# One decode step of attention with a gated MLP: how the K cache is laid over the 128 partitions, and what the score matmuls read

## The chip, the cores and the metric

The kernel runs on one core of one Trainium2 chip. The metric is device time in microseconds (us) of one execution, lower is better. The time of the kernel before is the median of three runs. Besides, one execution was recorded by the hardware profiler; its span is counted from the first to the last instruction of the core, and its own device time is a little longer than its span.

The names of the engines are those of the profile: PE is the matrix engine, PEld its weight loads, DVE the vector engine, ACT the scalar engine, POOL the GpSimd engine, and SP the engine that here only issues DMAs. A DMA is carried out by up to 16 DMA engines of the core, each of which works through its share of the DMAs in the order in which they were issued on a queue.

## The reference, cut to what matters

Two inputs x of width 448 (a batch of 2, one token each) are normalised, and then

```python
W = 2048                                    # the last 2048 of 8192 cached positions
q = (xn @ wq)                               # 16 heads of 256; each K/V head serves 2 of them
scores = einsum("bhqd,bhkd->bhqk", q, k) * 256 ** -0.5
p = softmax(scores)
s = einsum("bhqk,bhkd->bhqd", p, v) reshaped to 4096, @ wo
g = silu(relu(xn @ w1) @ w2)
out = x + s * g
```

All arrays are bf16. There are 2 batches with 8 K/V heads each, and of each the K and the V window is 2048 x 256, or 1 MB. K and V are 33.6 MB of the 44.1 MB that the kernel reads. Each number read is used for a handful of multiplications.

## The kernel before, in words

**Units.** The 16 pairs of batch and K/V head are handled in four units `u`; a unit has one batch and 4 heads, so 4 MB of K and 4 MB of V. `unit_src` (L197) describes the source of a unit: the 2048 positions of a head are cut into 32 blocks `kb` of 64 positions, and a row of 32 KB is one block of one head. The rows are listed as "kb h (t d)": the outer count is 32 blocks, the inner one 4 heads. So partition p of the SBUF buffer holds block p div 4 of head p mod 4. One DMA loads K of a unit (`load_k`, L279), one loads V (`load_v`, L282). The DMAs go out through `_Prog.dma` (L37), so in the profile all their issues have line L37.

**From K to scores.** `do_T` (L312) transposes K on DVE in four pieces of 128 x 2048 words of 4 bytes (a word is two bf16); the transposition is done in blocks of 32 x 32 words (L315). What was the partition within a group of 32 becomes the column within a block of 32 words. `do_S` (L318) then computes the scores of the unit with 32 matmuls: 8 parts `gp` of the head dimension by 4 heads `h`. The four heads write to four groups of 32 output rows, so that four matmuls can be in the array side by side. The moving operand of one matmul is 512 columns, picked from the transposed tile: 64 steps of 256 elements (`TS`), and within each 8 elements. With the order "block, head" within 32 partitions, the 8 blocks of one head stand 4 words, 16 bytes, apart.

**The rest of a unit.** `ch_max` (L330) finds the maximum over the scores and takes the exponential on ACT, `ch_spread` redistributes the result with 16 matmuls, `ch_pt` builds the weights on DVE, `do_PV` (L363) multiplies with V in 32 matmuls, also four side by side, whose moving operand is contiguous. `do_o_pe`, `do_at_exp` and `do_at` turn the output of the unit into columns for the last product.

**Buffers and what waits for them.** There are two buffers for K (`kbuf`), two for the transposed K (`kt`), and one for V (`vbuf`). `wq` is loaded into `kt[1]`, `w1` and `w2` into `kt[0]` once the scores of unit 2 are done, V of unit 2 into `kbuf[0]`, and `wo` into `kbuf[1]` in five parts. Each engine executes its own list in the order in which it is written out by hand from L466 on. The list of SP, which is the order of the large DMAs, is: wq, K0, K1, V0, K2 (waits for the transposes of unit 0), K3 (for those of unit 1), V1 (for the product with V0), V2 (for the transposes of unit 2), w1 (for the scores of unit 2), V3 (for the product with V1), w2, and five parts of wo (for the transposes of unit 3). SP stands at a DMA until its wait is over, and what is behind it on SP waits too. x is read by two small DMAs that ACT issues: `x_sb` as 2 rows, and `x_c` (L204) as 8 rows of 224 bytes, whose source is listed as 4 quarters by 2 batches. The output goes back in the same form of 8 rows (L549).

**The end.** The output product with `wo` is done in 32 steps on PE (L532 to L544) as the parts of wo land, after which two DVE instructions make the output, and one DMA writes it.

Of the kernel before, what the change touches and what calls it, by code (L numbers as in the profile page):

```python
# [12 lines left out]
PE, DVE, ACTE, SP, POOL = "pe", "dve", "act", "sp", "pool"  # L13
# [68 lines left out]
def bass_recurrent_scan__sliding_block_cached__dense_activation_relu__decode_kernel(  # L82
# [12 lines left out]
    _, HKV, SK, DH = A_k_cache.shape  # L95
# [3 lines left out]
    W = min(4096, max(256, SK // 4))  # L99
# [5 lines left out]
    HU = 4  # L105
    TS = 64
# [10 lines left out]
    with es:  # L117
        pr = _Prog(nc, es)

        def named(name, shape, dt):  # L120
            return es.enter_context(nc.sbuf_tensor(name, shape, dt))
# [4 lines left out]
        def view(t, off, dims, n=128, p0=0, pstep=1):  # L126
            width = t.shape[1]
            return bass.AP(t, p0 * width + off, [[width * pstep, n]] + dims)
# [40 lines left out]
        kbuf = [named(f"kbuf{i}", [128, UW], BF) for i in range(2)]  # L169
        vbuf = named("vbuf", [128, UW], BF)  # L170
        kt = [named(f"kt{i}", [128, UW], BF) for i in range(2)]
# [14 lines left out]
        def mm(out_ap, lhsT, rhs, start, stop=False, **kw):  # L186
            return lambda e: e.matmul(out_ap, lhsT=lhsT, rhs=rhs, start=start, stop=stop,  # L187
                                      skip_group_check=True, **kw)
# [8 lines left out]
        def unit_src(u, cache):  # L197
            hf, b = divmod(u, 2)
            return cache[b, HU * hf:HU * hf + HU, SK - W:SK, :].rearrange("h (kb t) d -> kb h (t d)", t=TS)
# [12 lines left out]
        d_k, d_v = {}, {}  # L212
# [64 lines left out]
        st = {}  # L277

        def load_k(u, deps=()):  # L279
            d_k[u] = pr.dma(SP, kbuf[u % 2][:, :], unit_src(u, A_k_cache), deps)  # L280

        def load_v(u, deps=()):  # L282
            d_v[u] = pr.dma(SP, vhome[u][:, :], unit_src(u, A_v_cache), deps)
# [27 lines left out]

        def do_T(u, c):  # L312
            src, dst = kbuf[u % 2][:, :].bitcast(F32), kt[u % 2][:, :].bitcast(F32)
            deps = [d_k[u], st.get(("S", u - 2))] + ([st["q_mm"]] if u == 1 else [])
            st["T", u] = pr.op(DVE, lambda e: e.transpose(  # L315
                dst[:, 2048 * c:2048 * c + 2048], src[:, 2048 * c:2048 * c + 2048]), deps)

        def do_S(u):  # L318
            deps = [st["T", u], st["q"], st.get(("exp", u - 2)), *st["q_n"]]
            for gp in range(NG):  # L320
                for h in range(HU):
                    lo = (u * NG + gp) * 32 + 8 * h
                    o = pr.op(PE, mm(sbk[u % 2][32 * h:32 * h + 8, :], q_big[:, lo:lo + 8],
                                     view(kt[u % 2], 64 * (gp // 2) + gp % 2 + 2 * h, [[256, TS], [8, 8]]),
                                     gp == 0, gp == NG - 1, tile_position=(0, 32 * h)), deps)
                    deps = []
            st["S", u] = o
# [136 lines left out]


        load_k(0)  # L466
        load_k(1)
        do_q()
        for c in range(4):
            do_T(0, c)  # L470
        do_S(0)
        load_v(0)
        load_k(2, [st["T", 0]])
        for c in range(3):
            do_T(1, c)
        ch_max(0)
        ch_spread(0)
        do_T(1, 3)
        load_k(3, [st["T", 1]])
        ch_pt(0)  # L480
        do_PV(0)
        load_v(1, [st["PV", 0]])
        do_S(1)
        for c in range(3):
            do_T(2, c)
# [5 lines left out]
        do_o(0)  # L491
        ch_pt(1)
        do_S(2)
        for c in range(3):
            do_T(3, c)
# [35 lines left out]
        deps = [st["at", 3], st["fs"]]  # L531
        for j in range(32):  # L532
            deps = deps + [d_wo.get(j)]
            if j < WO_TILED:
                m_o = tiled(j, at2[:, 32 * j:32 * j + 17], wo_sb[:, j * D:(j + 1) * D], WO_TILED, deps)
                deps = []
# [3 lines left out]
            for i in range(4):  # L540
# [3 lines left out]
                deps = []  # L544
# [36 lines left out]
```

## Time and profile before

| what | value |
|---|---|
| time, median of 3 runs (lowest, highest) | 112.09 us (111.26, 112.58) |
| the profiled execution: its device time | 111.33 us |
| the profiled execution: its span | 109.9 us |
| mean granted clock of PE, as a share of full speed | 0.812 |
| HBM read, and its mean rate over the span | 44.11 MB, 402 GB/s |
| PE busy, DVE busy, ACT busy | 62%, 54%, 11% of the span |

How to read it: the profiled execution is 0.76 us under the median of the three runs, and 1.43 us of its device time lie outside the span. "Busy" adds up the instructions of an engine; matmuls that run side by side are pipelined, so a busy PE says only that at least one is under way. In the timeline each row is a group of instructions of one line: the start, the busy time of the group, the engine, the line, the operation, output and inputs, shape, count, and in brackets the idle time just before it with what ended it. In the DMA view a packet is one contiguous run moved by one DMA engine, here one row of a partition, or the 4 bytes with which a DMA engine reports that its share of a DMA is done.

### The profile page before, as it was taken

Reading aid. Unit: us, or ns where it says so; the run is one execution under the profiler, and the core shown is the slowest. Engines: PE = TensorE matmul, PEld = TensorE weight load, DVE = VectorE, ACT = ScalarE, POOL = GpSimd, SP = SyncE. Lnnn points to the kernel's source line nnn. Section 1 sums busy time; section 2 is a strip of 40 time slices with the busy share of each in tenths; the row PEclk is TensorE's granted clock in tenths of the full one; section 3 lists DMA queues with packets and bytes.
Section 4 is the critical chain, followed back from the end, with each engine's and each line's share of the span. In section 5 each row is a group of like instructions: output and inputs, shape, how many; then the busy total and the mean of one; then the engine's idle time right before and its main releaser. Section 6 shows DMA issues by size and latency. Waiting matters only on the chain.

```text
span 109.9 us, 1131 instructions
## 1 busy us (share of the span) xinstructions
PE 68.5 (62%) x490; PEld 23.3 (21%) x469; DVE 59.8 (54%) x84; ACT 12.2 (11%) x21; POOL 4.4 (4%) x14
## 2 busy tenths in 40 slices
PE   0010699500001995579995699989999892556871
PEld 0000001000000110553110622146213841211330
DVE  2167000399999996825984879995005026003621
ACT  2930000340000000201000200040001300020000
POOL 7800000000000000000000000000000000000000
PEclk9999999995555599656999755999999999955555
DMA  6798998999899989989999999999899998999920
GB/s 168 334 460 388 513 430 382 418 489 430 382 501 441 394 382 525 430 382 406 483 430 394 430 489 406 394 477 447 344 425 496 453 406 363 413 433 417 413 115 1
DMA packets 2463, 44.16 MB, mean 402 GB/s; under 512 B 282, under 2 KB 412, under 8 KB 924
## 3 DMA queue, kind: packets, MB, share of 16 engines
q1 hardware_dynamic: 2432, 44.11, 94.3%
q8 instruction: 3, 0.05, 0.2%
q10 hardware_dynamic: 28, 0.01, 0.0%
HBM read 44.11 MB, written 0.00 MB: 402 GB/s over the span
## 4 chain that ended last, share of the span: by engine, by line
DMA 36%; PE 32%; DVE 26%; issue 2%; ACT 1%; SPq 0%
DMA kbuf<-in_A_wo_dram 26%; PE sp L187 23%; DVE kt L315 15%; DMA kt<-in_A_wq_dram 10%; PE sp L192 6%; DVE q_t L305 2%; DVE mx L332 2%; DVE q_big L307 2%; PE gbk L187 2%; ACT e_sb L339 1%; PE hbk L187 1%; DVE q_n L299 1%; DVE pt L356 1%; DVE mxt L334 1%; DVE nb L338 1%
## 5 line engine op out<-in xcount | busy, mean ns | idle before, releaser
L187 PE MATMUL sp<-kt,q_big 128*8 128x512 bf16 x128 | 30.1, 1088 | 14.4 <-DVE kt L315 14.4
L315 DVE STREAM_TRANSPOSE kt<-kbuf 128x2048 f32<-128x2048 f32 x16 | 35.6, 2274 | 2.8 <-DMA kbuf<-in_A_k_cache_dram 2.7
L187 PEld LDWEIGHTS sp<-kt,q_big 128*8 128x8 bf16 x128 | 4.7, 103 | 34.0 <-issue 18.4
L187 PE MATMUL sp<-e_sb,sel 128*128 128x64 bf16 x64 | 8.1, 294 | 5.3 <-ACT e_sb L339 5.3
L187 PE MATMUL sp<-vbuf,pt 128*16 128x512 bf16 x96 | 8.0, 492 | 2.4 <-DMA vbuf<-in_A_v_cache_dram 1.9
L187 PEld LDWEIGHTS sp<-e_sb,sel 128*128 128x128 bf16 x64 | 7.0, 119 | 8.2 <-ACT e_sb L339 8.2
L339 ACT ACTIVATE e_sb<-sp,nb 128x512 bf16<-128x512 f32 x4 | 2.8, 688 | 51.5 <-DVE nb L338 51.5
L332 DVE TENSOR_REDUCE mx<-sp 128x1 f32<-128x512 f32 x4 | 2.7, 687 | 9.4 <-PE sp L187 9.4
L192 PE MATMUL sp<-kt,xr 128*128 128x512 bf16 x21 | 7.7, 488 | 0.0
L299 DVE TENSOR_SCALAR q_n<-sp 128x1024 bf16<-128x1024 f32 x1 | 1.2, 1225 | 10.5 <-PE sp L192 10.5
L187 PE MATMUL sp<-kt,xr 128*128 128x512 bf16 x7 | 3.6, 512 | 3.7 <-DMA kt<-in_A_wq_dram 3.7
L187 PE MATMUL mbk<-ident,xg 2*128 2x2 bf16 x7 | 0.3, 163 | 7.9 <-DVE xg L237 7.9
L356 DVE TENSOR_TENSOR pt<-sp,hmask 128x512 bf16<-128x512 f32 x4 | 2.8, 698 | 4.2 <-PE sp L187 4.2
L387 DVE TENSOR_TENSOR at_exp<-mbk,qmask 128x64 bf16<-128x64 f32 x4 | 0.8, 204 | 7.2 <-PE mbk L187 7.2
L187 PEld LDWEIGHTS sp<-vbuf,pt 128*16 128x16 bf16 x96 | 3.1, 120 | 7.0 <-DMA vbuf<-in_A_v_cache_dram 3.7
L372 ACT ACTIVATE o_sb<-sp 128x512 bf16<-128x512 f32 x4 | 2.4, 593 | 17.9 <-PE sp L187 17.9
L399 DVE TENSOR_SCALAR at<-mbk,rs 64x32 bf16<-64x32 f32 x4 | 1.4, 350 | 3.6 <-PE mbk L187 3.6
L187 PEld LDWEIGHTS sp<-kt,xr 128*128 128x128 bf16 x7 | 0.8, 121 | 10.7 <-issue 6.9
L187 PE MATMUL gbk<-kbuf,at 128*17 128x448 bf16 x24 | 3.0, 570 | 0.1
L302 ACT ACTIVATE q_n<-sp 128x1024 bf16<-128x1024 f32 x1 | 1.0, 1024 | 14.5 <-PE sp L192 14.5
L187 PE MATMUL gbk<-kt,h_sb 128*17 128x448 bf16 x14 | 1.7, 569 | 1.3 <-DMA kt<-in_B_w_dram 1.3
L305 DVE STREAM_TRANSPOSE q_t<-q_n 128x2048 bf16<-128x2048 bf16 x1 | 2.3, 2311 | 0.0
(74 smaller groups left out, 45.8 us busy)
## 6 DMA issues: line engine op xcount, KB each, us to landing
kbuf<-in_A_k_cache_dram SPq DMA_DIRECT2D x4, 4096.0 KB, 17.9
vbuf<-in_A_v_cache_dram SPq DMA_DIRECT2D x3, 4096.0 KB, 21.6
kbuf<-in_A_v_cache_dram SPq DMA_DIRECT2D x1, 4096.0 KB, 18.7
kt<-in_A_wq_dram SPq DMA_DIRECT2D x1, 3584.0 KB, 11.2
kt<-in_B_w_dram SPq DMA_DIRECT2D x2, 1568.0 KB, 19.3
kbuf<-in_A_wo_dram SPq DMA_DIRECT2D x2, 1120.0 KB, 27.3
kbuf<-in_A_wo_dram SPq DMA_DIRECT2D x1, 672.0 KB, 29.3
kbuf<-in_A_wo_dram SPq DMA_DIRECT2D x1, 448.0 KB, 29.1
```

What stands on the lines that cost most here:

```text
L187: return lambda e: e.matmul(out_ap, lhsT=lhsT, rhs=rhs, start=start, stop=stop, skip_group_check=True, **kw)
L192: return lambda e: e.add_instruction(mybir.InstMatmult(name=nc.get_next_instruction_name(), start_tensor_calc=start, stop_tensor_calc=stop ...
L299: e.tensor_scalar(out=view(q_n, 0, [[64, 16], [32, 2], [1, 32]]), in0=view(sp, 0, [[64, 16], [1, 2], [2, 32]]), scalar1=SCALE, scalar2=Non ...
L305: v = pr.op(DVE, lambda e: e.transpose(q_t[:, :], q_n[:, :]), halves)
L307: st["q"] = pr.op(DVE, lambda e, qd=qd: e.tensor_copy(view(q_big, qd, [[NG * 32, NU], [32, NG], [4, 8]], n=32, p0=32 * qd), view(q_t, 0, [ ...
L315: st["T", u] = pr.op(DVE, lambda e: e.transpose(dst[:, 2048 * c:2048 * c + 2048], src[:, 2048 * c:2048 * c + 2048]), deps)
L332: v = pr.op(DVE, lambda e: e.tensor_reduce(out=mx[:, 0:1], in_=sbk[k], axis=AX.X, op=ALU.max), [st["S", u], p_mx, st.get("mxt")])
L334: v = st["mxt"] = pr.op(DVE, lambda e: e.transpose(mxt[:, :], mx[:, :]), [v, st.get("neg")])
L339: st["exp", u] = pr.op(ACTE, lambda e: e.activation(e_sb[k][:, :], sbk[k], ACT.Exp, bias=nb[k][:, 0:1], accum_out=ssum[k][:, 0:1]), [v, st ...
L356: st["pt", u] = pr.op(DVE, lambda e: e.tensor_tensor(out=view(pt[u % 2], 0, [[128, 4], [1, 128]]), in0=view(sp, 1024, [[0, 4], [1, 128]]), ...
L372: st["osb", u] = pr.op(ACTE, lambda e: e.activation(o_sb[:, :], obk[:, :], ACT.Copy), [o, st.get(("oT", u - 1))])
L399: st["at", u] = st["mbk"] = pr.op(DVE, lambda e: e.tensor_scalar(out=view(at2, 16 * b, [[32, 32]], n=64, p0=p0), in0=mbk[p0:p0 + 64, 32:64 ...
```

## The change

K of a unit is loaded by four DMAs in place of one, each to 32 partitions. Within each quarter of 32 partitions the order is now head, then block: partition 32 q + 8 h + j holds block 8 q + j of head h. The transposes wait for all four. The score matmuls pick the columns accordingly: the 8 blocks of one head stand 1 word, 4 bytes, apart, and heads 8 words apart. The bytes that are loaded, the number of matmuls and their shapes, the transposes, V and everything behind the scores stay as they are.

```diff
         def load_k(u, deps=()):
-            d_k[u] = pr.dma(SP, kbuf[u % 2][:, :], unit_src(u, A_k_cache), deps)
+            hf, b = divmod(u, 2)
+            src = A_k_cache[b, HU * hf:HU * hf + HU, SK - W:SK, :].rearrange("h (q kb t) d -> q h kb (t d)", q=4, t=TS)
+            d_k[u] = [pr.dma(SP, kbuf[u % 2][32 * q:32 * q + 32, :], src[q], deps) for q in range(4)]
...
         def do_T(u, c):
             src, dst = kbuf[u % 2][:, :].bitcast(F32), kt[u % 2][:, :].bitcast(F32)
-            deps = [d_k[u], st.get(("S", u - 2))] + ([st["q_mm"]] if u == 1 else [])
+            deps = [*d_k[u], st.get(("S", u - 2))] + ([st["q_mm"]] if u == 1 else [])
...
                     o = pr.op(PE, mm(sbk[u % 2][32 * h:32 * h + 8, :], q_big[:, lo:lo + 8],
-                                     view(kt[u % 2], 64 * (gp // 2) + gp % 2 + 2 * h, [[256, TS], [8, 8]]),
+                                     view(kt[u % 2], 64 * (gp // 2) + gp % 2 + 16 * h, [[256, TS], [2, 8]]),
                                      gp == 0, gp == NG - 1, tile_position=(0, 32 * h)), deps)
```

The source of one such DMA, `src[q]`, is listed as 4 heads by 8 blocks by a row of 32 KB: its outer count is 4. That of the one DMA before, from `unit_src`, is 32 blocks by 4 heads by a row of 32 KB: its outer count is 32.

## The prediction

> **What bounds the kernel now.** I read the page's slices and DMA queues first, then stretches of the span, then the DMA view of short windows, and last the timeline around the scores. The slices and queues of the page:
>
> ```profile
> PEclk9999999995555599656999755999999999955555
> DMA  6798998999899989989999999999899998999920
> ...
> DMA packets 2463, 44.16 MB, mean 402 GB/s; under 512 B 282, under 2 KB 412, under 8 KB 924
> ...
> q1 hardware_dynamic: 2432, 44.11, 94.3%
> ...
> q10 hardware_dynamic: 28, 0.01, 0.0%
> ```
>
> The mean share of the 16 DMA engines is 0.8 or more from the third slice to the last but two. By stretches (start to end, length, busy time of PE, PEld, DVE, ACT, POOL, then PE clock, DMA share, GB/s) it is plainer:
>
> ```profile
> 26.00:36.00 10.00, 0.71 (x4) 0.10 (x8) 9.97 (x6) 0.00 (x0) 0.00 (x0) 0.50 0.98 423
> 52.00:62.00 10.00, 7.87 (x43) 1.85 (x36) 8.26 (x8) 1.03 (x3) 0.00 (x0) 0.99 1.03 441
> 62.00:72.00 10.00, 10.00 (x66) 3.37 (x68) 8.86 (x10) 0.00 (x0) 0.00 (x0) 0.67 1.02 439
> ```
>
> PE is idle in the first and full in the last of these, and the DMA engines are full in all three: they set the pace. The timeline gives the price of one load:
>
> ```profile
> 11.96 0.61 PE L187 MATMUL sp<-kt,xr 128*128 128x512 bf16 x1 [3.71 <-DMA kt<-in_A_wq_dram]
> ...
> 50.65 6.70 DVE L315 STREAM_TRANSPOSE kt<-kbuf 128x2048 f32<-128x2048 f32 x3 [2.72 <-DMA kbuf<-in_A_k_cache_dram]
> ```
>
> PE waited for wq until 11.96, DVE for K2 until 50.65. Between them the engines moved K0, K1, V0 and K2, four loads of 4.19 MB: 38.7 us, or **9.67 us a load**, which is 27.1 GB/s for each of 16 engines.
>
> How many engines a load uses shows in its completion packets. A window that holds the end of just one load, K1 (25 to 35 us):
>
> ```profile
> DMA packets 144, 4.19 MB, mean 419 GB/s; under 512 B 16, under 2 KB 16, under 8 KB 16
> ```
>
> That is 128 rows and 16 packets under 512 B: 16 engines each reported their share. The small loads that ACT issues, on queue q10, in windows of their own: `x_sb` (0 to 2 us), `x_c` (5 to 10 us), the output (108 to 110 us):
>
> ```profile
> q10 hardware_dynamic: 4, 0.00, 0.3%
> ```
>
> ```profile
> q10 hardware_dynamic: 12, 0.00, 0.2%
> ```
>
> ```profile
> q10 hardware_dynamic: 12, 0.00, 0.5%
> ```
>
> `x_sb` has 2 rows, so 2 completions. `x_c` and the output have 8 rows each, so 4 completions, not 8: **four engines took 2 rows each**. Their DRAM side is listed as 4 quarters by 2 batches. So the outer count of the DRAM side, 4, set the number of engines, although 8 rows would divide among 8. For K it was 32 (blocks), and 16 took part. It adds up over the page: q1 has 2176 rows in 16 DMAs, and 2176 + 16 x 16 = 2432; q10 has 18 + 2 + 4 + 4 = 28.
>
> **The change part by part.** The sum is made against the profiled execution (span 109.9 us, device time 111.33 us), which stands 0.76 us under the median of the runs.
>
> *K in four DMAs.* The DRAM side of each is listed as 4 heads by 8 blocks by 32 KB: its outer count falls from 32 to 4, as in `x_c`. I expect four engines per DMA. At 27.1 GB/s an engine, 1.05 MB on four engines takes 1.05 / (4 x 27.1 GB/s) = 9.67 us: as long as the whole unit takes on 16. What four such DMAs cost together depends on which engines they get, which no row shows. Lower bound: a fresh four for each, so that all 16 work side by side, 9.67 us a unit, no loss. Upper bound: the same four each time, 4 x 9.67 = 38.7 us a unit. I take the upper: `x_c` and the output came out with the same four completions 100 us apart, so the count follows from the instruction alone; the plainest way to pick the engines is then also without memory, and a rotation would need one. It is an inference. [...]
>
> The extra is 38.7 - 9.67 = 29.0 us a unit, 116.1 us for four. Does the kernel wait for all of it? On the four engines everything stands in one line: wq, K0, K1, V0, K2, K3, V1, V2, w1, V3, w2, wo, since their shares of V and of the weights still wait behind K. Landings, from 11.96 in steps of 38.7 (K) and 9.67 (V): K0 50.6, K1 89.3, V0 99.0, K2 137.7, K3 176.4, V1 186.0, V2 195.7; then w1, V3, w2 about 199.5, 209, 213. Each issue must come before the line runs dry. K2 waits for four transposes (4 x 2.27 us) after K0: 60, dry at 99. K3 after those of unit 1: about 100, dry at 137.7. V1 after the product with V0 (3.6 us): about 104, dry at 176. V2 after the transposes of unit 2: 148, dry at 186. V3 after the product with V1: 189, dry at 199.5, the nearest. wo after the transposes of unit 3: 187. So no gap opens, the four engines are never idle, and all 116.1 us lie on the path. The other 12 engines stand idle about half the time.
>
> *Twelve more issues on SP.* A load's issue takes 0.54 us; 12 are 6.5 us. K1 to V0 start up to 3.3 us later, while wq and K0 keep the engines until 21 us or later. K2 and K3 each end 1.6 us later: the least slack now is at K3, whose issue ends by 46.98 in SP's timeline while K2 lands at 50.65, so 3.7 us cover it. Cost 0; with the cover gone, 1.6 us each. The wait for four completions rather than one on DVE: under 0.1 us by the 0.02 us between dependent steps in the chain. Nothing else is moved past a queue; behind the transposes on DVE stand `ch_max` and the next unit's, which have their 10 us.
>
> *The scores.* They are the part that does get cheaper. From the timeline, scores and product with V, at half clock and at full:
>
> ```profile
> 35.29 7.47 PE L187 MATMUL sp<-kt,q_big 128*8 128x512 bf16 x32 [14.44 <-DVE kt L315]
> ...
> 48.00 3.62 PE L187 MATMUL sp<-vbuf,pt 128*16 128x512 bf16 x32 [0.56 <-DVE rs L360]
> ...
> 75.70 7.51 PE L187 MATMUL sp<-kt,q_big 128*8 128x512 bf16 x32
> ```
>
> ```profile
> 83.28 1.93 PE L187 MATMUL sp<-kbuf,pt 128*16 128x512 bf16 x32
> ```
>
> Both are 32 matmuls of 512 columns, four abreast. The product with V follows the clock (3.62 to 1.93 us); the scores do not (7.47 and 7.51): what holds them is reading columns 16 bytes apart. At 4 bytes I expect between 7.5 (no gain) and the contiguous 1.93 to 3.62 us, nearer the latter: 3.9 to 5.6 us a unit, 16 to 22 us of PE time. Worth on the path: 0, because loads cover it. Even before the change no load was issued later for want of it by more than the backlog; in the changed kernel the last scores (after K3 at 176 and its transposes) end 25 us before the last part of wo lands. With that cover gone it would be worth up to 22 us, but the cover is 10 us of load per unit at the least.
>
> *The end.* What follows the last part of wo is unchanged, 2.9 us. The four engines may end up to 2 us before or after the slowest of now, since instruction loads delay single engines.
>
> Sum: span 109.9 + 116.1 = 226.0; device time 111.33 + 116.1 = **227.4 us**, rounded 227.5. About twice the time before.
>
> **The rivals.**
> *A, not slower: the four DMAs of a unit spread over all 16 engines* (a different four each, or each over 16). For it: nothing here shows which four `x_c` took. Against it: `x_c` did stop at four engines, with eight rows to share out. Then loads land as now, PE gets freer, and the end stays tied to the 44.1 MB: 111.3 us, at best some 0.5 us less from the stretches with a share of 0.95. It decides if a unit of K lands 9.7 us after its predecessor.
> *B: all of K at half rate.* 32 partitions are a quarter of the destination; if two engines share a way into them, or if 8 engines take part, a unit takes 19.35 us: 4 x 9.67 = 38.7 more, span 148.6, device time 150.0. For it: no load here goes to fewer than 128 partitions in bulk, so nothing excludes it. Against: `x_c` speaks for four. It decides if units of K land 19 us apart. [...]
> *C: worse than the forecast*: the four engines also get in each other's way in the 32 partitions. If two share a way, 77.4 us a unit: 227.4 + 154.8 = 382 us. Against it: in no window of the trace do loads run visibly below the 27.1 GB/s an engine.
>
> **How the numbers follow.** Four engines, the same ones: 0.81, 227.5 us. A: 0.10. B: 0.06. C and others slower: 0.03. The range 222 to 232 holds the first: 2 us for the end, 1.6 us each for two late issues, and 1% for the run against the profile; the other three leave out 0.19. A measurement of this kernel can tell about 1% from no change. Faster by over 1%: 0.03, from A if more hangs on PE than I see; within 1%: 0.07, the rest of A; slower: 0.90.
>
> **What the profile would show.** Right: the loads of K have 4 completions each (one load's window of 32 rows has 4 packets under 512 B); the DMA share falls to about 0.25 in long stretches, at some 108 GB/s; DVE waits for K in every unit, nearly 40 us apart; the scores take 2 to 4 us a unit and the time doesn't care; PE's clock is low for most of the span. Wrong: DMA share near 1 with K landing every 9.7 us (A), or a share of 0.5 to 1 with K every 19 us (B). The step likeliest to fail is which four engines are taken.

## The result and the profile after

The changed kernel takes **259.54 us** (median of 4 runs, 259.04 to 259.78), against 111.68 us for the kernel before (median of 4 runs, three of which are those shown above). The ratio is 2.32, with a 95% interval of 2.304 to 2.338. The forecast was 227.5 us, in a range of 222 to 232. So the direction, and most of the loss, came as forecast, but 32 us of it did not. The profiled execution took 259.5 us, with a span of 257.9 us: 31.9 us above the 226.0 us of the forecast.

The slices and queues of the page after:

```profile
PEclk9999555555575555568555555566555555688675
DMA  7759872222222222239982222299985222499951
GB/s 281 330 163 239 168 183 102 117 107 102 117 107 102 117 107 102 117 135 219 244 173 102 102 107 117 102 234 203 239 175 139 112 102 107 180 406 395 422 238 43
DMA packets 2463, 44.16 MB, mean 171 GB/s; under 512 B 282, under 2 KB 412, under 8 KB 924
...
q1 hardware_dynamic: 2432, 44.11, 53.2%
```

The same bytes in the same number of packets: four times the loads of K, each with a quarter of the completions. There are two kinds of slices that the kernel before does not have. In one the share of the DMA engines is 0.2 and 102 to 117 GB/s flow: a quarter of the engines work at their full pace. In the other the share is 0.8 or more and yet only 168 to 244 GB/s flow: all engines are busy, at about half their pace. A window that holds one load of a quarter of K (51 to 60.7 us) shows the first kind:

```profile
DMA packets 36, 1.05 MB, mean 108 GB/s; under 512 B 4, under 2 KB 4, under 8 KB 4
...
q1 hardware_dynamic: 36, 1.05, 25.0%
```

32 rows and 4 completions in 9.7 us: four engines, 27 GB/s each, as forecast. Stretches of the changed kernel, with the columns of the stretches shown before the change (the last three are PE clock, DMA share, GB/s):

```profile
18.00:37.00 19.00, 3.73 (x16) 0.29 (x3) 5.31 (x6) 2.31 (x2) 0.00 (x0) 0.69 0.97 207
42.00:60.00 18.00, 0.00 (x0) 0.00 (x0) 0.00 (x0) 0.00 (x0) 0.00 (x0) 0.50 0.25 109
117.00:136.00 19.00, 0.00 (x0) 0.00 (x0) 0.00 (x0) 0.00 (x0) 0.00 (x0) 0.60 0.93 200
170.00:190.00 20.00, 2.43 (x28) 0.54 (x16) 0.05 (x1) 0.00 (x0) 0.00 (x0) 0.59 0.98 209
```

The first, third and fourth are the second kind: there V0, V1 and V2 run on the other 12 engines while K runs on its four. Behind V2 the 12 engines go on to w1, still beside K3: from 190.5 to 197 us the share is 0.90 and 194 GB/s flow. A packet of 32 KB takes 1.21 us when a unit of K runs by itself, and mostly 2.2 to 2.6 us on all 16 engines in these stretches. The timeline of the transposes, each of which starts when its K has landed:

```profile
60.77 8.89 DVE L317 STREAM_TRANSPOSE kt<-kbuf 128x2048 f32<-128x2048 f32 x4 [33.59 <-DMA kbuf<-in_A_k_cache_dram]
99.41 6.70 DVE L317 STREAM_TRANSPOSE kt<-kbuf 128x2048 f32<-128x2048 f32 x3 [29.75 <-DMA kbuf<-in_A_k_cache_dram]
...
157.70 6.70 DVE L317 STREAM_TRANSPOSE kt<-kbuf 128x2048 f32<-128x2048 f32 x3 [46.61 <-DMA kbuf<-in_A_k_cache_dram]
...
210.09 6.70 DVE L317 STREAM_TRANSPOSE kt<-kbuf 128x2048 f32<-128x2048 f32 x3 [40.04 <-DMA kbuf<-in_A_k_cache_dram]
```

K1 lands 38.6 us after K0: this unit ran alone, and cost just what was forecast. K2 lands 58.3 us after K1, of which 9.7 us are V0's share in the line, so 48.6 us; K3 lands 52.4 us after K2. K0 took 48.2 us from the landing of wq, for which PE waited until 12.57 us in this execution. Against 38.7 us each, that is 9.5, 0, 9.9 and 13.7 us more, 33.1 us for the four (K3 has w1 beside it as well as V2). wq landed 0.6 us later than before the change, and the end gave 1.8 us back: 31.9 us.

The scores did get faster:

```profile
69.72 3.58 PE L187 MATMUL sp<-kt,q_big 128*8 128x512 bf16 x32 [47.99 <-DVE kt L317]
114.34 1.91 PE L187 MATMUL sp<-kt,q_big 128*8 128x512 bf16 x32
168.99 3.44 PE L187 MATMUL sp<-kt,q_big 128*8 128x512 bf16 x32
225.38 1.90 PE L187 MATMUL sp<-kt,q_big 128*8 128x512 bf16 x32
```

They take 1.9 us at full clock (1.00 in 225.4 to 227.2 us) and 3.4 to 3.6 us at 0.50 to 0.54, about as long as the product with V. PE stands idle for 48 us in front of the first of them, and for 35 to 50 us in each of the units behind.

### The profile page after: what moved, and what is told of

Same layout as the page of the kernel before. It is cut to its first block, busy times and chain, and to the rows that moved or that the text cites. A ratio compares the mean times of both kernels' runs of the same rounds, so it can differ in the third digit from the quotient of the medians.

```text
span 257.9 us, 1151 instructions
## 1 busy us (share of the span) xinstructions
PE 52.0 (20%) x490; PEld 22.0 (9%) x469; DVE 59.8 (23%) x84; ACT 12.4 (5%) x21; POOL 4.4 (2%) x14
## 4 chain that ended last, share of the span: by engine, by line
another core or an unknown queue 52%; DMA 29%; DVE 10%; PE 6%; SPq 1%; issue 1%; ACT 1%; DVEq 0%
DMA kbuf<-in_A_k_cache_dram 19%; DMA kbuf<-in_A_wo_dram 10%; DVE kt L317 8%; PE sp L187 4%; SPq L37 1%; PE gbk L187 1%; ACT e_sb L341 1%; PE hbk L187 1%; DVE mx L334 0%; DVE pt L358 0%; DVE fs L444 0%; DVE mxt L336 0%; DVE nb L340 0%; DVE nbt L337 0%
## 5 line engine op out<-in xcount | busy, mean ns | idle before, releaser
L187 PE MATMUL sp<-vbuf,pt 128*16 128x512 bf16 x96 | 10.6, 618 | 51.1 <-DMA vbuf<-in_A_v_cache_dram 50.6
L187 PE MATMUL sp<-kt,q_big 128*8 128x512 bf16 x128 | 10.8, 496 | 48.0 <-DVE kt L317 48.0
L187 PEld LDWEIGHTS sp<-kt,q_big 128*8 128x8 bf16 x128 | 3.3, 99 | 54.5 <-DVE kt L317 49.1
L374 ACT ACTIVATE o_sb<-sp 128x512 bf16<-128x512 f32 x4 | 2.4, 597 | 27.1 <-PE sp L187 27.1
L187 PE MATMUL sp<-kbuf,pt 128*16 128x512 bf16 x32 | 2.9, 519 | 1.9 <-DMA kbuf<-in_A_v_cache_dram 1.9
L187 PE MATMUL gbk<-kbuf,at 128*17 128x448 bf16 x24 | 2.4, 473 | 1.3 <-DMA kbuf<-in_A_wo_dram 1.3
L309 DVE COPY q_big<-q_t 32x256 bf16<-32x256 bf16 x4 | 1.8, 443 | 0.1
```

The lines of the kernel that those rows point to most:

```text
L309: st["q"] = pr.op(DVE, lambda e, qd=qd: e.tensor_copy(view(q_big, qd, [[NG * 32, NU], [32, NG], [4, 8]], n=32, p0=32 * qd), view(q_t, 0, [ ...
L374: st["osb", u] = pr.op(ACTE, lambda e: e.activation(o_sb[:, :], obk[:, :], ACT.Copy), [o, st.get(("oT", u - 1))])
```

## The experiments

The runs have short names here, e1 to e4 and f1 to f7. e1 and e4 were run ten and four times, the others once each; the repeated runs of one kernel lie within 1.2% of each other (111.26 to 112.58 us for the kernel before, 259.04 to 259.78 us for the changed one). The diffs show the lines that matter; those with plus signs alone stand in place of the lines of the change, and `....rearrange` stands for the slice of `A_k_cache`, which stays as it is.

**The two halves of the change, each alone (e1, e2).** e1: the new columns with the old loads.

```diff
-view(kt[u % 2], 64 * (gp // 2) + gp % 2 + 2 * h, [[256, TS], [8, 8]])
+view(kt[u % 2], 64 * (gp // 2) + gp % 2 + 16 * h, [[256, TS], [2, 8]])
```

> The loads of the kernel before, with the column pattern of the changed scores (it picks columns that belong to mixed heads; only its time counts). Theory: the loads set the end and the scores are covered. Then the scores of a unit fall from 7.5 us to between 1.9 and 3.6 us, and the time stays within 1% of the kernel before, 110.5 to 112.5 us. Rival: the scores hang on the path after all, as the chain of waits with its 23% for PE seems to say. Then the time falls by at least one unit's saving, 4 us, to 107 us or less.

Measured: 111.3 us against 111.12 us, ratio 1.0017, interval 0.9995 to 1.0039: no difference. The scores of its timeline:

```profile
34.05 3.59 PE L187 MATMUL sp<-kt,q_big 128*8 128x512 bf16 x32 [14.43 <-DVE kt L315]
48.98 1.91 PE L187 MATMUL sp<-kt,q_big 128*8 128x512 bf16 x32
63.19 3.28 PE L187 MATMUL sp<-kt,q_big 128*8 128x512 bf16 x32
77.01 3.19 PE L187 MATMUL sp<-kt,q_big 128*8 128x512 bf16 x32
```

Some 18 us of PE time are gone (12.0 us in place of 30) and the time is the same. What the change is about is worth nothing here, because the loads of 44 MB set the end. e2: the other half, the new loads with the old columns (the diff of `load_k` and `do_T` without that of `do_S`):

> The loads of the changed kernel, with the old column pattern (again mixed heads). Theory: the whole loss is in the loads, and the four DMA engines that carry K never run dry, so slower scores cost nothing: 258 to 261 us. Rival: the faster scores already bring part of it; then it is slower than the changed kernel by 4 to 16 us, 263 to 276 us.

Measured: 259.31 us, against 259.54 us for the changed kernel, with scores of 7.4 to 7.6 us a unit. So the whole loss is in the loads, and the slower scores cost nothing there either.

**Is it the count or the 32 partitions (e3)?** A way, in what follows, is a path that DMA engines are supposed to share when they write into a group of partitions; no trace shows it itself. One load per unit to all 128 partitions, whose source has an outer count of 4:

```diff
-src = ....rearrange("h (q kb t) d -> q h kb (t d)", q=4, t=TS)
-d_k[u] = [pr.dma(SP, kbuf[u % 2][32 * q:32 * q + 32, :], src[q], deps) for q in range(4)]
+src = ....rearrange("h (kb t) d -> h kb (t d)", t=TS)
+d_k[u] = [pr.dma(SP, kbuf[u % 2][:, :], src, deps)]
```

> K of a unit by one DMA to all 128 partitions, whose source is listed as 4 heads by 32 blocks (the scores read mixed heads). Theory: the number of engines follows from the outer count 4 alone, so four completions per load, K alone at 108 GB/s, a unit of K in 38.7 us or more, and a time of 227 to 262 us, the upper end if the doubled packets beside V remain. Rival: what matters is that a load reaches only 32 partitions. Then this load to 128 partitions has all 16 engines and the time is 111 to 115 us. A second rival, two engines sharing a way into partitions 32 or 64 apart: K alone at 54 GB/s, a unit in 77 us, about 380 us.

Measured: 328.57 us, which none of the three had named. The loads do have four completions, as the count says. The page of its profile counts 2176 rows, 12 loads with 16 completions and the four loads of K with 4 each, 2384 in all:

```profile
q1 hardware_dynamic: 2384, 44.11, 47.0%
```

So the rival of 32 partitions falls. But K by itself does not reach 108 GB/s. Stretches in which K is alone on the engines:

```profile
40.00:76.00 36.00, 0.00 (x0) 0.00 (x0) 0.00 (x0) 0.00 (x0) 0.00 (x0) 0.50 0.25 61
...
260.00:290.00 30.00, 1.31 (x16) 0.51 (x20) 10.07 (x8) 0.78 (x2) 0.00 (x0) 0.50 0.24 100
```

The share says that four engines are at work in both; they move 61 GB/s early and 100 GB/s late. By share and rate, a row of 32 KB took some 2.2 us on average in the early stretch and 1.3 us in the late one. Which rows an engine takes, no trace gives; if each takes a run of consecutive rows, the four write 32 partitions apart from each other. That two engines share a way and meet less as they drift apart would explain both; that was argued, not tried. The second rival had this mechanism, and its 380 us supposed that they never drift. So the count alone does not set the time. Where engines are in each other's way, 32 partitions apart or 64, this run does not tell; f3 below, where K on partitions 0 to 63 keeps its full pace beside V0 (433 GB/s), speaks for 32 if V0 is written to 64 to 127 in that time.

**Half of the partitions, 16 engines (e4).** An order that keeps pairs of blocks together, so that the outer count is 16:

```diff
+src = ....rearrange("h (g two t) d -> two g h (t d)", two=2, t=TS)
+d_k[u] = [pr.dma(SP, view(kbuf[u % 2], 0, [[1, UW]], n=64, p0=i, pstep=2), src[i], deps) for i in range(2)]
...
+view(kt[u % 2], 64 * (gp // 2) + gp % 2 + 4 * h, [[256, TS], [16, 4], [2, 2]])
```

> Another order within the 32 partitions: pair of blocks, head, block in the pair. K of a unit by two DMAs of 64 partitions two apart, whose source is listed as 16 pairs by 4 heads. The scores read two columns 4 bytes apart, then a gap. Theory: outer count 16, so 16 engines, a unit of K in 9.7 us, and the time of the kernel before within 1%, 110.5 to 112.5 us, with scores of 2 to 5 us a unit. Rival: half of the partitions is what makes a load slow: then a unit takes up to 19.4 us and the time is up to 150 us.

Measured: 151.74 us, ratio 1.366, interval 1.361 to 1.372: the rival, and a little over its 150. All 16 engines are busy and move half:

```profile
14.00:44.00 30.00, 9.49 (x54) 1.63 (x37) 14.20 (x10) 2.31 (x2) 0.00 (x0) 0.66 0.99 211
```

The rival's reason does not hold, though: f7 below loads a quarter of the partitions at a time and moves the same 210 GB/s. Engines that share ways two by two would give half in both; for e4 that is argued, not tried.

**Which engines, and is it source or destination (f1 to f6)?** First (f1), the stretches with V beside K were taken away, by more waits:

```diff
-load_v(0)
+load_v(0, d_k[1])
...
-load_v(1, [st["PV", 0]])
+load_v(1, [st["PV", 0], *d_k[3]])
...
-load_v(2, [st["T", 2]])
+load_v(2, [st["T", 2], *d_k[3]])
```

> The changed kernel, with V0 held back until K1 has landed and V1 and V2 until K3 has landed, so that no load of V runs beside a load of K. Theory: the 32 us by which the changed kernel is over the forecast are the three stretches in which the other 12 engines run ahead with V and every packet takes double. Then all packets of 32 KB take 1.21 us and the time is the forecast plus about 2 us for each of two restarts of the queue, 228 to 234 us. Rival: the extra is in the loads of K by themselves; then it stays at 255 us or more, and holding V back makes it longer still.

Measured: 232.33 us, with a span of 230.9 us. In place of the stretch of 18 to 37 us at 0.97 and 207 GB/s:

```profile
18.00:37.00 19.00, 1.82 (x9) 0.10 (x1) 5.31 (x6) 2.31 (x2) 0.00 (x0) 0.61 0.26 110
...
104.00:170.00 66.00, 10.26 (x99) 4.67 (x91) 11.12 (x12) 1.38 (x3) 0.00 (x0) 0.55 0.25 109
```

K runs at 109 to 110 GB/s, and K1 and K3 land 38.7 us after K0 and K2 (transposes from 50.39, 89.10, 140.06 and 178.76 us). So letting 12 engines rest makes the kernel 27 us faster: the 32 us over the forecast are the price of V, and of w1 behind it, running beside K. Holding V back has a price of its own, which covers the 4.9 us over 226.0: V0 and V1 land 12.5 and 12.4 us after the K before them, in place of 9.67. No run shows the 2 us a restart that were expected; measured here are 2.8 and 2.7 us.

Next (f2), K read from rows 320 KB apart in place of 4 MB:

```diff
+src = [A_k_cache[b, HU * hf + q, 0:40 * TS, :].rearrange("(h kb t) d -> h kb (t d)", h=4, t=TS)[:, 0:8, :] for q in range(4)]
```

> The changed kernel with another source for K (other rows of the cache, so only its time counts): the four groups of rows that the four engines read side by side lie 320 KB apart and not 4 MB. Destinations, engines and counts are unchanged. Theory of destination: the doubling beside V comes from where the rows are written. Then nothing changes, 256 to 262 us. Theory of source: it comes from reading rows a large power of two apart. Then the packets beside V take 1.21 us and the time is 226 to 232 us.

Measured: 260.11 us, and in the stretch of 18 to 37 us all engines are still busy at half their pace:

```profile
18.00:37.00 19.00, 2.84 (x14) 0.20 (x2) 5.31 (x6) 2.31 (x2) 0.00 (x0) 0.66 0.94 200
```

The distance of the rows in DRAM is not it, nor which rows of the cache K is read from.

Then a pair of kernels that differ in nothing but the order of the four loads. f3: quarters in the old order of rows, whose outer count is 8, with the old columns in `do_S`:

```diff
-...rearrange("h (q kb t) d -> q h kb (t d)", q=4, t=TS)
+...rearrange("h (q kb t) d -> q kb h (t d)", q=4, t=TS)
```

> Four loads per unit as in the change, but in the old order, block and then head, so that a quarter's source is listed as 8 blocks by 4 heads; the scores read 16 bytes apart again. Engine count: 8 completions per load, a unit of K in 19.4 us, and 150 us if nothing runs slower beside V. Theory of destination: while V0 runs ahead on the other eight engines, K0 is written to partitions 0 to 63, and if those have their own ways in, packets take 1.21 us in this stretch (12 to 21 us). Theory of source: packets double here too, 170 to 180 us.

and f4, the same with the order reversed:

```diff
-for q in range(4)]
+for q in (3, 2, 1, 0)]
```

> The kernel with eight engines, its four quarters loaded in the reverse order, so that V0 runs beside the quarters 96 to 127 and 64 to 95 of K0. Sources and engine counts are the same. Theory of destination: the eight engines that run ahead with V write their own 64 partitions, 64 to 127, so now every packet in the stretch from 12 us on takes double, 2.4 us, and the kernel is slower than with the quarters in order, by 5 to 30 us. Theory of source: no difference between the two orders beyond 2 us.

Measured: 165.85 us in order, 161.6 us reversed. In this window, three loads of the kernel in order (36.4 to 50.9 us, K alone), there are 96 rows and 24 completions, so 8 engines a load:

```profile
DMA packets 120, 3.15 MB, mean 217 GB/s; under 512 B 24, under 2 KB 24, under 8 KB 24
```

The stretch that the pair was made for, V0 beside the first quarters of K0, in order and reversed:

```profile
12.00:21.00 9.00, 8.55 (x28) 0.78 (x7) 0.41 (x1) 0.41 (x1) 0.00 (x0) 1.00 1.01 433
```

```profile
12.00:21.00 9.00, 8.49 (x28) 0.80 (x7) 0.21 (x1) 0.21 (x1) 0.00 (x0) 1.00 1.03 211
```

The engine counts, the busy shares and the distances between the rows that are read are the same: 433 GB/s while K goes to partitions 0 to 63, and 211 GB/s while it goes to 64 to 127. The rows read are other ones too, since a quarter's rows go with its partitions, but f2 had moved the rows under unchanged destinations without effect. The theory of source falls. That the eight engines that run ahead with V write partitions 64 to 127, where K then collides with them, fits both stretches; which partitions an engine writes, no trace gives. Over the whole kernel the expected sign was wrong: in order, it is V1 and V2 that meet the upper quarters (1.03 and 222 GB/s in 72 to 86 us, 0.99 and 210 GB/s in 102 to 112 us), whereas reversed they meet mostly the lower ones (0.83 and 315, 0.94 and 396 GB/s), so that the reversed kernel is 4.3 us faster.

Last, back to four engines, with eight loads of 16 partitions a unit, in two orders (the columns of the scores follow). f5:

```diff
+src = ....rearrange("h (q kb t) d -> q h kb (t d)", q=8, t=TS)
+d_k[u] = [pr.dma(SP, kbuf[u % 2][16 * q:16 * q + 16, :], src[q], deps) for q in (4, 0, 2, 1, 3, 5, 6, 7)]
...
+view(kt[u % 2], 64 * (gp // 2) + gp % 2 + 8 * h, [[256, TS], [32, 2], [2, 4]])
```

> Still four engines for K, but in eight loads of 16 partitions a unit, in the order 64, 0, 32, 16, 48, 80, 96, 112 of the first partition (the order of rows within 32 partitions and the columns of the scores follow). When V0 sets out on the other 12 engines, some 17 us in, K0 is on partitions 0 to 15, then on 32 to 47. Theory of destination: these are the ways of the four engines themselves, which V's other 12 engines do not use. Then packets take 1.21 us for both in the first stretch of V0 (17.5 to 25 us), and the time falls below the changed kernel, to 232 to 252 us, by how many of the later stretches are spared. Rival, any load of V beside any load of K on four engines doubles: 257 to 263 us.

and f6, with `for q in (4, 1, 3, 0, 2, 5, 6, 7)`, so that K0 is on partitions 16 to 31 and 48 to 63 when V0 was expected to set out. If some of V's streams meet K's there, either those alone slow down, or all 16 do:

> [...] Theory of hold-up: where some streams share a way, all 16 streams are held up and every packet takes double, as in the changed kernel. Time 240 to 265 us in either case; the packets of the stretch from 17.5 us on decide.

Measured: 255.98 us and 233.47 us, the other way round than expected, and both outside the times that their theories gave. Both expectations had V0 set out at 17.5 us, as in the changed kernel. It set out at 24 us, since SP had 16 loads to issue before it (13.8 us) and then took 8.4 us for V0's issue. By then K0 was past its second and third load: from 26 us on it wrote partitions 16 to 31 and 48 to 63 in the first kernel, and 0 to 15 and 32 to 47 in the second. The stretch of 27 to 34 us in the first and in the second:

```profile
27.00:34.00 7.00, 0.00 (x0) 0.00 (x0) 0.00 (x0) 0.00 (x0) 0.00 (x0) 0.50 1.05 220
```

```profile
27.00:34.00 7.00, 0.00 (x0) 0.00 (x0) 0.00 (x0) 0.00 (x0) 0.00 (x0) 0.50 1.01 435
```

So the theories behind the pair, read after the fact, fit the partitions that were really written: with K on 0 to 15 and 32 to 47, four engines of K and 12 of V run at full pace side by side (435 GB/s at a share of 1.01). With K on 16 to 31 and 48 to 63, the packets of 32 KB take 2.5 us by share and rate (220 of 435 GB/s), so all 16 streams slow down, as in the theory of hold-up; with eight of them at half pace some 326 GB/s would have been left. Which of V's streams K's four meet there, no trace shows.

**Rival B by itself (f7).** 32 partitions a load, with a contiguous source, so that 16 engines take part:

```diff
+src = [A_k_cache[b, HU * hf + q, SK - W:SK, :].rearrange("(p t) d -> p (t d)", t=TS) for q in range(4)]
```

> K by four loads of 32 partitions a unit, but the source of each is one contiguous run of 32 rows (one head a quarter; the scores read mixed heads), so that 16 engines can take part. It measures rival B of the prediction alone. Engine count alone: 16 completions a load, a unit of K in 9.7 us, 111 to 113 us. Theory of destination: two of the 16 engines share each way into 32 partitions, packets of K take 2.4 us, a unit 19.4 us, 148 to 153 us.

Measured: 154.74 us, a little over the 148 to 153 of the theory of destination and the 150.0 of rival B. Each load of 1 MB has 16 completions, and all engines are busy at half the pace, as in this stretch:

```profile
14.00:44.00 30.00, 10.26 (x53) 1.51 (x37) 14.20 (x10) 2.31 (x2) 0.00 (x0) 0.68 1.00 210
```

So both losses that the prediction weighed against each other exist. 16 engines on 32 partitions move 210 GB/s, half of the 423 to 441 GB/s that 16 engines move in the stretches of the kernel before; 4 engines on 32 partitions, with nothing beside them, keep their 27 GB/s each (108 to 109 GB/s).

## Why the prediction was right in kind and wrong in size

- *What bounds the kernel:* right. Faster scores alone change nothing (111.3 against 111.12 us, e1), and slower ones cost nothing (e2).
- *Four engines per load, from the outer count:* right, and read from 12 packets of a load of 1.8 KB. Outer counts of 4, 8 and 16 or more gave 4, 8 and 16 completions (the changed kernel, f3, e4 and f7).
- *The same four each time:* right, as far as the runs can tell. It was an inference; K1's four loads landed one after the other, 38.6 us for the unit, where 9.67 us would have shown a fresh four for each. No trace gives the engines' numbers.
- *No gap in the line of the four engines:* right. V3, the nearest, was issued at 223.3, before V2 landed at 229.3.
- *"At 27.1 GB/s an engine ... 38.7 us a unit":* **the step that failed.** It took the pace of an engine as its own, whatever the others do. It is right for K1, but K0, K2 and K3 took 48.2, 48.6 and 52.4 us, because the 12 engines that were said to "stand idle about half the time" do their shares of V first (and of w1, beside K3), and in that time all 16 go at half pace. The term was 116.1 us and measured 149.2 (33.1 more); f1, which keeps V away from K, came to a span of 230.9 us against the 226.0 us of the sum.
- *Rivals B and C* each supposed two engines that share a way into the partitions, which fits the halved pace, but only among the engines of one load, and C was given up because "in no window of the trace do loads run visibly below the 27.1 GB/s an engine". That was no evidence: in the kernel before every load covers 128 partitions, and 98% of its packets of 32 KB take 1.21 us, so that its trace could not show two engines meeting. Within one load e3 (61 of 108 GB/s) and f7 (210 of 435 GB/s) show a loss. The same question should have been asked of the loads that run at the same time: the changed kernel beside V0 (207 GB/s) and f5 (220 GB/s) show it there.
- *Twelve issues on SP at no cost:* right for the time, but not in kind. V0's issue took 9.3 us (6.75 to 16.1) with K0 and K1 queued ahead of it. It made the end no later, as V0's place in the line was behind both.
- *The scores, 1.9 to 3.6 us:* right. The row from 35.29 us that stands there for half clock had a mean clock of 0.82, but the reading holds: in the same trace the scores took 7.51 us both in the row from 63.68 us, at 0.67, and in that from 75.70 us, at 1.00. What columns 16 bytes apart cost is shown by e1, where 4 bytes take 1.91 to 3.59 us.
- *The end, up to 2 us either way:* right, 1.8 us came back there. That instruction loads delay single engines shows in the trace before: three packets of 16 KB took 0.89 to 0.96 us, and the packets of 32 KB right behind them 1.68 to 1.76 us in place of 1.21.

What stays open is why all the streams are held up and not some: in f5 V0 goes to 128 partitions and K at that time to 32, and all 16 streams halve (220 of 435 GB/s). The runs show the hold-up; what causes it was not tried.

## What to carry to other kernels

Before you reshape a DMA, look at the outer count of its DRAM side, and count the completion packets of a load of that form, even a tiny one: in these runs outer counts of 4, 8 and 16 or more went with 4, 8 and 16 completions (the changed kernel, f3, e4 and f7). Then try which partitions can be written at the same time, over all loads in flight and not load by load, because beside V0 K on partitions 16 to 31 and 48 to 63 halved all sixteen streams (220 GB/s, f5), and K on 0 to 15 and 32 to 47 none (435 GB/s, f6). And ask first what the bound is: 18 us of saved matmul time were worth nothing to a kernel whose DMA engines were full.

## What the runs showed of the hardware that was not expected

- Running less at a time can be faster: holding V back until K has landed, so that 12 of 16 engines rest, took the changed kernel from 259.5 to 232.3 us.
- Reading a moving operand of 2-byte elements, 32 matmuls of 512 columns four abreast: 7.4 to 7.6 us with each element 16 bytes from the next (e2 and the kernel before, there at mean clocks from 0.67 to 1.00); 3.8 to 4.0 us with pairs of elements 4 bytes apart, one pair every 32 bytes (e4), also at clocks of 0.96 and 1.00; 1.9 us with runs of eight elements 4 bytes apart, at full clock (the changed kernel and e1), the same as the 1.93 us of the product with V, whose operand is contiguous.
- An issue on SP can itself take long: 9.3 us for V0 behind eight loads of K on four engines in the changed kernel, where those of V1, V2 and V3 took 0.55 to 0.58 us. Behind eight loads of K on eight engines it took 0.6 us (f3).
